# An attention and SwiGLU layer on one core: matmuls of the next stage placed at the seams between stages, and the last output block in two halves

## The chip, the cores and the metric

The kernel runs on one core of one Trainium2 chip. The metric is device microseconds of one execution, as the median of several. Single executions of one kernel differ by up to 5 us here, so the argument rests on two things: timed runs in the same rounds, and the waits of TensorE (PE in the profile) at the seams between the stages, which repeat to about 0.01 us from trace to trace.

## The reference

A transformer block on one sequence of 2,048 tokens with width 1,024, in bfloat16. In short:

```python
mod = (silu(c) @ w_mod)                       # sa, ca, ga, sb, cb, gb
h = layernorm(x) * (1 + ca) + sa
x = x + ga * attention(h)                     # 32 query heads, 4 key/value heads, dim 128,
                                              # the last 512 cached positions, output product with wo
h = layernorm(x) * (1 + cb) + sb
x = x + gb * ((silu(h @ w_gate) * (h @ w_up)) @ w_down)   # inner width 3584
```

## The kernel before

The sequence is worked in two halves (`sc` 0 and 1) of 1,024 tokens, in four stages: attention of half 0, its output product, the same for half 1; then, for each half, rounds of gate-up products and the down product. The large products are done with seven half-size products instead of eight (a Strassen scheme); "product 1" to "product 7" below are these. That needs sums of weights and of activations beforehand, and VectorE (DVE) makes them. A bank is one of the buffers that matmuls add their result into; before it is used anew, ScalarE or VectorE has to empty it. A central helper records every operation, so nearly all matmuls carry one line number (L272) in the profile; the tile names and the time tell them apart.

One attention step is: a part of the query product, the scores of the step before, the exponential on ScalarE (ACT), the product with the values of two steps before, another part of the query product. The seam to the output stage is the last lines:

```python
for i in range(lo, hi + 2):
    ...
    q_first_half(sc, i)              # q products 3, 7, 4, 5 of a group, by i % 4
    scores(i - 1)                    # 4 matmuls of 512 columns; then 2 exponentials of 1024
    pv(i - 2)                        # 16 matmuls of 129 columns
    q_second_half(sc, i)             # q products 2, 1, 6 of the next group
    ...
    if i == hi - 6: start_o(sc)                     # loads output weights, rows 0 to 13
    if i >= hi - 1:                                 # three steps: hi-1, hi, hi+1
        n = 5 * (i - hi + 1)
        for j in range(2):
            o_early(sc, j, n, min(n + 5, 14))       # output rows ahead: 10, 10, 8 matmuls
```

The query products are made in groups of seven, one group for four steps. At the start of the second attention half the products 2, 1, 5, 6 of its first group were made inside the output stage, and product 3 in the first step:

```python
def o_hook0(idx, j):                 # after each column j of output product idx
    ...
    if idx == 6:
        if j == 2:  q_step(1, 0, 2); q_step(1, 0, 1)
        next(hs[0])                                  # activation sums, 1.22 us each on VectorE
        ...
        if j == 3:  q_step(1, 0, 5); q_step(1, 0, 6)
```

A gate-up round (`q` the new weight pair, `pq` the one before). `gmm(bank, n, ...)` is product n, four matmuls; `snap` copies a bank on ScalarE; `g_sum`, `u_sum` add two products on VectorE; `ws(n)` makes n weight sums on VectorE:

```python
if a: gmm(ga, 1, wg); gmm(gb_, 2, wg); snap(sn0, gb_)
if b: gmm(xb, 3, vg); snap(sn1, xb)
if a:
    g_sum(q, 0, ga, sn0)
    if q % FP < 2: ws(2)
if b: gmm(zb, 3, vu); snap(sn2, zb); g_sum(pq, 2, xa, sn1)
if a: g_act(q, 0); gmm(ua, 1, wu); gmm(ub, 2, wu)    # g_act: SiLU on ScalarE
if b: u_sum(pq, 2, za, sn2); g_act(pq, 2)
if a: snap(sn0, ub)
if b: gmm(xa, 7, vg); ...
if a:
    u_sum(q, 0, ua, sn0)
    if q % FP < 2: ws(2)
if b: gmm(za, 7, vu); ...
if a: u_mul(q, 0); ws(2); gmm(ga, 6, wg); gmm(gb_, 5, wg); ...
if b: ...; gmm(xa, 4, vg); ...
if a: gmm(ua, 6, wu); ...
```

The first round of a half has only the `a` lines, the last round only the `b` lines. So in these two rounds, little other work lies between a product and the next product that needs its bank emptied. The weight sums of a half began with its first round (`wsum[0] = w_sums(q0)`). The last block of 512 output columns ended with a multiplication and an addition on VectorE, and then its store.

The softmax here doesn't subtract the row's maximum and nothing guards it: scores larger than these inputs give would overflow.

## Time and profile before

| before | value | where it is read |
|---|---|---|
| median of the first 3 runs | 1167.37 us (1165.66 to 1170.86) | times |
| span of the profiled run | 1164.3 us | page |
| PE busy | 1148.6 us, 99% | page |
| granted PE clock | 1.000 | list of cores |
| matmuls of 512 columns, start to start | 216 ns | trace, consecutive matmul starts |

The page of the kernel before: span, busy time of each engine with its share and its number of instructions, and the shares of the chain of work that ended last.

```profile
span 1164.3 us, 18217 instructions
...
PE 1148.6 (99%) x7087; PEld 585.3 (50%) x7087; DVE 818.1 (70%) x1638; ACT 529.4 (45%) x739; POOL 68.9 (6%) x136
...
PE 91%; DVE 3%; DMA 3%; SPq 1%; ACT 1%; issue 1%; POOL 0%; DVEq 0%; ACTq 0%; POOLq 0%
```

TensorE is the limit. VectorE, the next one, has 30% idle. So only the time that TensorE idles, plus the start and the end, can be won. The waits of PE in the kernel before, in total us, times, and longest:

```profile
PE ps L272 <- POOL arena L406: 2.2, 1, 2.2
PE ps L272 <- DVE arena L829: 2.2, 5, 0.6
PE ps L272 <- ACT arena L799: 2.0, 5, 0.5
PE ps L272 <- DVE arena L821: 1.8, 2, 1.4
PE ps L272 <- DVE arena L900: 1.6, 3, 0.6
```

L829 is an addition that empties a bank, L799 the exponential, L900 a weight sum. To place the waits one goes to the timeline of PE, one line per run of matmuls: start, length, engine, operation, count, and in brackets the idle time before it. First the end of the first attention half:

```profile
236.80 1.45 PE L272 MATMUL ps<-arena 128*128 128x129 bf16 x17
238.76 1.40 PE L272 MATMUL ps<-arena 128*128 128x512 bf16 x16 [0.51 <-ACT arena L799]
```

The scores wait for the exponential. The idle time shown is 0.51 us, but the true loss is larger. The profile models a 512-column matmul as 379 ns long, while they follow each other every 216 ns. The loss is therefore the idle time plus 0.16, that is 0.67 us. All waits in this document, unless said otherwise, are such losses: the spacing of two starts less the usual spacing for that width. Small losses don't break a line of the timeline of PE; there the weight loads (PEld) show them.

The start of the second half, where product 7 waits for an addition:

```profile
342.72 2.10 PE L272 MATMUL ps<-arena 128*128 128x512 f16 x9
345.38 2.43 PE L272 MATMUL ps<-arena 128*128 128x512 f16 x10 [0.55 <-DVE arena L829]
```

The first gate-up round, all engines:

```profile
650.55 0.60 ACT L832 ACTIVATE nsc<-ps 128x512 f32<-128x512 f32 x1 [28.76 <-PE ps L272]
...
651.16 1.28 ACT L1511 ACT_TABLE_LOAD   x1
651.18 0.69 DVE L829 TENSOR_TENSOR arena<-ps,nsc 128x512 f16<-128x512 f32 x1 [0.94 <-PE ps L272]
651.79 0.87 DVE L900 TENSOR_TENSOR arena<-arena 128x512 f16<-128x512 bf16 x2
652.46 0.63 ACT L1511 ACTIVATE arena<-arena 128x512 f16<-128x512 f16 x1
...
652.72 1.90 PE L272 MATMUL ps<-arena 128*128 128x512 f16 x8 [0.48 <-DVE arena L900]
652.99 0.58 ACT L832 ACTIVATE nsc<-ps 128x512 f32<-128x512 f32 x1
653.60 0.69 DVE L829 TENSOR_TENSOR arena<-ps,nsc 128x512 f16<-128x512 f32 x1 [0.94 <-ACT nsc L832]
...
655.14 1.04 PE L272 MATMUL ps<-arena 128*128 128x512 f16 x4 [0.53 <-DVE arena L900]
```

Two waits for weight sums (L900). Behind the second stands another limit: ScalarE loads SiLU's table for 1.28 us, then does the SiLU and a copy, and only then VectorE can add, until 654.29. The last gate-up round of the first half, PE:

```profile
813.67 2.61 PE L272 MATMUL ps<-arena 128*128 128x512 f16 x11
816.76 3.58 PE L272 MATMUL ps<-arena 128*128 128x512 f16 x15 [0.48 <-DVE arena L829]
```

The first gate-up round of the second half (called the twin below), PE:

```profile
909.21 2.48 PE L272 MATMUL ps<-arena 128*128 128x512 f16 x10 [0.58 <-DVE arena L900]
```

And the tail, VectorE:

```profile
1160.82 0.69 DVE L1100 TENSOR_TENSOR tmp<-ps,rowb 128x512 f32<-128x512 f32 x1 [1.60 <-PE ps L272]
1161.55 0.69 DVE L1107 TENSOR_TENSOR arena<-tmp,x_res 128x512 bf16<-128x512 f32 x1
```

### The profile page before, as it was taken

Reading aid. Unit: us, or ns where it says so; the run is one execution under the profiler, and the core shown is the slowest. Engines: PE = TensorE matmul, PEld = TensorE weight load, DVE = VectorE, ACT = ScalarE, POOL = GpSimd, SP = SyncE. Lnnn points to the kernel's source line nnn. Section 1 sums busy time; section 2 is a strip of 40 time slices with the busy share of each in tenths; the row PEclk is TensorE's granted clock in tenths of the full one; section 3 lists DMA queues with packets and bytes.
Section 4 is the critical chain, followed back from the end, with each engine's and each line's share of the span. In section 5 each row is a group of like instructions: output and inputs, shape, how many; then the busy total and the mean of one; then the engine's idle time right before and its main releaser. Section 6 shows DMA issues by size and latency. Waiting matters only on the chain.

```text
span 1164.3 us, 18217 instructions
## 1 busy us (share of the span) xinstructions
PE 1148.6 (99%) x7087; PEld 585.3 (50%) x7087; DVE 818.1 (70%) x1638; ACT 529.4 (45%) x739; POOL 68.9 (6%) x136
## 2 busy tenths in 40 slices
PE   9899999999999999999999999999999999999998
PEld 5565556654446666656444444444444444444443
DVE  4857997657567777686657798777558777776535
ACT  3766777730117777787100354454110444444010
POOL 1100221000000111111000010000000000000000
PEclk9999999999999999999999999999999999999999
DMA  9779899797816888835775332423774423233343
GB/s 331 171 186 200 220 211 223 177 189 203 245 37 148 197 194 205 201 94 130 173 201 163 87 94 73 109 73 100 208 193 151 118 75 107 73 105 129 128 154 109
DMA packets 289765, 179.98 MB, mean 155 GB/s; under 512 B 130448, under 2 KB 277904, under 8 KB 289680
## 3 DMA queue, kind: packets, MB, share of 16 engines
q1 hardware_dynamic: 226736, 92.31, 36.1%
q10 hardware_dynamic: 54304, 55.05, 14.9%
q0 software_dynamic: 8640, 31.46, 8.9%
q8 instruction: 56, 0.92, 0.4%
q14 instruction: 29, 0.24, 0.1%
HBM read 128.45 MB, written 19.92 MB: 127 GB/s over the span
## 4 chain that ended last, share of the span: by engine, by line
PE 91%; DVE 3%; DMA 3%; SPq 1%; ACT 1%; issue 1%; POOL 0%; DVEq 0%; ACTq 0%; POOLq 0%
PE ps L272 91%; DMA arena<-arena 1%; DMA x_res<-in_A_x_dram 1%; DVE arena L829 1%; DMA arena<-in_A_wo_dram 1%; DVE st L413 1%; SPq L382 0%; DVE arena L900 0%; DMA wo_sum<-arena 0%; SPq L341 0%; ACT arena L799 0%; SPq L364 0%; DVE arena L821 0%; ACT nsc L832 0%; SPq L310 0%
## 5 line engine op out<-in xcount | busy, mean ns | idle before, releaser
L272 PE MATMUL ps<-arena 128*128 128x512 f16 (+2 forms) x6782 | 1141.4, 330 | 11.9 <-POOL arena L406 2.2
L272 PEld LDWEIGHTS ps<-arena 128*128 128x128 bf16 (+1 forms) x6782 | 575.0, 98 | 570.6 <-DVE arena L829 9.4
L799 ACT ACTIVATE arena<-ps 128x1024 bf16<-128x1024 f32 x256 | 261.0, 1021 | 49.1 <-PE ps L272 37.2
L832 ACT ACTIVATE tmp<-ps 128x512 f32<-128x512 f32 x166 | 99.1, 597 | 300.8 <-PE ps L272 286.7
L900 DVE TENSOR_TENSOR arena<-arena 128x512 f16<-128x512 bf16 x328 | 133.1, 418 | 3.1
L829 DVE TENSOR_TENSOR arena<-ps,tmp 128x512 bf16<-128x512 f32 (+1 forms) x134 | 91.8, 685 | 46.5 <-PE ps L272 34.5
L821 DVE TENSOR_TENSOR arena<-ps,rl 128x512 f16<-128x512 f32 x128 | 88.5, 691 | 6.0 <-DMA arena<-arena 1.6
L832 ACT ACTIVATE nsc<-ps 128x512 f32<-128x512 f32 x84 | 50.1, 596 | 93.2 <-PE ps L272 90.9
L829 DVE TENSOR_TENSOR arena<-ps,nsc 128x512 f16<-128x512 f32 x84 | 57.3, 686 | 40.4 <-PE ps L272 31.1
L818 DVE RECIPROCAL rl<-ps 128x4 f32<-128x4 f32 x128 | 23.0, 179 | 87.6 <-PE ps L272 86.6
L1038 DVE TENSOR_TENSOR arena<-arena 128x2048 f16<-128x2048 f16 (+3 forms) x56 | 56.0, 1009 | 13.5 <-PE ps L272 12.9
L1511 ACT ACTIVATE arena<-arena 128x512 f16<-128x512 f16 x84 | 49.9, 624 | 30.7 <-DVE arena L829 30.7
L829 DVE TENSOR_TENSOR tmp<-ps,tmp 128x512 f32<-128x512 f32 x32 | 22.0, 689 | 56.4 <-ACT tmp L832 48.3
L832 ACT ACTIVATE arena<-ps 128x512 f32<-128x512 f32 x16 | 9.6, 597 | 93.4 <-PE ps L272 93.4
L950 DVE TENSOR_TENSOR arena<-arena 128x512 f16<-128x512 bf16 x120 | 47.8, 419 | 2.4 <-DMA arena<-in_A_wo_dram 1.4
L413 DVE BATCH_NORM_STATS2 st<-x_res 128x6 f32<-128x512 bf16 x60 | 40.9, 682 | 3.8 <-DMA x_res<-in_A_x_dram 3.4
L1526 DVE TENSOR_TENSOR arena<-arena 128x512 f16<-128x512 f16 x84 | 34.9, 415 | 0.2
L1106 DVE TENSOR_TENSOR tmp<-tmp,rowb 128x512 f32<-128x512 f32 x48 | 33.2, 692 | 1.6
L427 DVE TENSOR_SCALAR nsc<-x_res,mv,rstd 128x1024 f16<-128x1024 bf16 (+1 forms) x30 | 16.1, 538 | 25.2 <-DMA arena<-nsc 24.0
L594 DVE SCALAR_TENSOR_TENSOR arena<-arena 128x1024 bf16<-128x1024 bf16 x24 | 29.1, 1214 | 0.0
L1107 DVE TENSOR_TENSOR arena<-tmp,x_res 128x512 bf16<-128x512 f32 x32 | 22.1, 692 | 1.1
L829 DVE TENSOR_TENSOR arena<-ps,rowb 128x512 f16<-128x512 f32 x28 | 19.3, 689 | 3.9 <-ACT rowb L832 3.9
(86 smaller groups left out, 330.6 us busy)
## 6 DMA issues: line engine op xcount, KB each, us to landing
arena<-in_A_wq_dram SPq DMA_DIRECT2D x28, 512.0 KB, 5.2
arena<-wo_sum ACTq DMA_DIRECT2D x7, 2048.0 KB, 9.1
arena<-in_B_w_gate_dram SPq DMA_DIRECT2D x28, 512.0 KB, 4.0
arena<-in_B_w_up_dram SPq DMA_DIRECT2D x28, 512.0 KB, 5.0
arena<-wd_sum ACTq DMA_DIRECT2D x8, 1792.0 KB, 8.0
arena<-in_B_w_down_dram ACTq DMA_DIRECT2D x6, 1792.0 KB, 7.3
arena<-in_A_wo_dram POOLq DMA_DIRECT2D x16, 512.0 KB, 5.0
wo_sum<-arena POOLq DMA_DIRECT2D x16, 512.0 KB, 4.3
```

What stands on the lines that cost most here:

```text
L272: T.op(PE, lambda: TE.matmul(out_ap, lhsT, rhs, start=start, stop=stop, skip_group_check=skip), reads=reads, writes=[bank_buf])
L413: T.op(DVE, lambda: V.bn_stats(st_[sl][:, hf * 6:hf * 6 + 6], x_res[:, t, hf * 512:hf * 512 + 512]), reads=[B_x[t]], writes=[B_st[sl]])
L799: T.op(ACT, lambda: A.activation(ex_s[es][:, 2 * kp:2 * kp + 2, :], banks2(SCB + 2 * kp), AF.Exp, scale=att_scale), writes=[PB[SCB + 2 * k ...
L821: T.op(DVE, lambda: V.tensor_tensor(o_s[os_].rearrange("p (a b) d -> p a b d", a=2), psap(PVB * 512, [[512, 2], [130, 2], [1, P]]), rlb, A ...
L829: T.op(DVE, lambda: V.tensor_tensor(out, bank(ba), other, ADD), reads=[ob2], writes=[PB[ba], ob])
L832: T.op(ACT, lambda: A.activation(dst, bank(bk), AF.Copy), writes=[PB[bk], db])
L900: T.op(st, lambda: eng.tensor_tensor(o, a, b, op), reads=rd, writes=[wr])
L950: T.op(DVE, lambda: V.tensor_tensor(o, a, b, SUB), reads=rd, writes=[wr])
L1038: T.op(DVE, lambda: V.tensor_tensor(o, a, b, SUB), reads=rd, writes=[sb])
L1106: T.op(DVE, lambda: V.tensor_tensor(tm, tm, rw, MULT), reads=[B_row[row]], writes=[tb])
L1511: T.op(ACT, lambda: A.activation(o, s_, AF.Silu), reads=[sb], writes=[ob])
L1526: T.op(DVE, lambda: V.tensor_tensor(gu[blk][:, p, :], o, s_, MULT), reads=[sb, ob], writes=[B_gu[blk][p]])
```

## The change

The intent is to put matmuls that the next stage needs anyway into the gaps at the seams, and to shorten the tail. Five parts:

1. Attention ends: the 28 early output matmuls are spread over five steps rather than three (4 of them in two earlier steps), and the weights are loaded earlier, in smaller pieces.
2. Start of the second attention half: product 3 of its first group also moves into the output stage, and products 5 and 6 are made there one column earlier, straight after products 2 and 1.
3. First gate-up round of both halves: four weight sums move into the columns of the product before.
4. Last gate-up round of both halves: ten down matmuls are made early (`fill`).
5. The last block of output columns is computed in two halves of 256.

The core of the diff, with cuts:

```diff
             def q_first_half(sc, i):
                 c = i % 4
-                if c < 3:
+                if c < 3 and i != NI:
                     q_step(sc, group_at(sc, i - c), (3, 7, 4)[c])
                 else:
                     q_step(sc, group_at(sc, i + 1), 5)
 ...
-                    if i >= hi - 1:
-                        n = 5 * (i - hi + 1)
-                        for j in range(2):
-                            o_early(sc, j, n, min(n + 5, 14))
+                    if i >= hi - 3:
+                        n = i - hi + 3
+                        o_early(sc, 1, EARLY[1][n], EARLY[1][n + 1])
+                        o_early(sc, 0, EARLY[0][n], EARLY[0][n + 1])
+            EARLY = ((0, 0, 0, 4, 10, 14), (0, 2, 4, 7, 11, 14))
 ...                                                     # o_hook0, idx == 6, j == 2:
                         q_step(1, 0, 2)
                         q_step(1, 0, 1)
+                        q_step(1, 0, 5)
+                        q_step(1, 0, 6)
+                        q_step(1, 0, 3)
 ...                                                     # o_hook1, idx == 6:
+                    if j == 0:
+                        wsum[0] = w_sums(0)
+                    ws(1)
 ...                                                     # gate_up:
-                    if q % FP < 2:
+                    if q % FP == 1:
                         ws(2)
                 if b:
                     gmm(zb, 3, vu, False)
                     snap(*sn[2], zb)
                     g_sum(pq, 2, xa, sn[1])
+                    if fill:
+                        fill(0, 6)
 ...
                     gmm(za, 7, vu, False)
                     u_sum(pq, 3, za, tms[1])
                     g_act(pq, 3)
+                    if fill:
+                        fill(6, 10)
 ...                                                     # seven_products, last product:
+                    if halves and j == TPC - 1:
+                        lo, hi = slice(0, CH // 2), slice(CH // 2, CH)
+                        T.op(ACT, lambda: A.activation(sj[j][0][:, lo], bank(AB[j])[:, lo], AF.Copy), ...)
+                        prod(6, j, BB_[j], True, c=lo)
+                        out(1, j, 0, BB_[j], None, sj[j], lo)
+                        prod(6, j, AB[j], False, c=hi)
+                        out(1, j, 0, AB[j], None, None, hi)
```

More of the change, by code (lines that the diff above doesn't have):

```diff
@@ L1025, in _, with seven_products @@
             ORDER = (1, 2, 6, 5, 3, 7, 4)
-            def seven_products(nk, X, XBf, offs, s1, ver, AB, BB_, out, sj, own_s1, hook, early=(0,) * 4):
+            def seven_products(nk, X, XBf, offs, s1, ver, AB, BB_, out, sj, own_s1, hook, early=(0,) * 4, halves=False):
                 S = {n: [_Buf("S%d_%d" % (n, j)) for j in range(TPC)] for n in (2, 3, 4)}
@@ L1038, in inplace, with prod @@
                         T.op(DVE, lambda: V.tensor_tensor(o, a, b, SUB), reads=rd, writes=[sb])
-                def prod(idx, j, bk, start, k0=0, k1=nk):
+                def prod(idx, j, bk, start, k0=0, k1=nk, c=slice(0, CH)):
                     n = ORDER[idx]
@@ L1049, in prod @@
                             lb = XBf[x][k] if n in (1, 2, 4) else S[{6: 2, 3: 4, 7: 3}[n]][j]
-                        mm(bank(bk), la, va, start and k == 0, k == nk - 1, [lb, vb], PB[bk], skip=True)
+                        mm(bank(bk)[:, c], la, va[:, c], start and k == 0, k == nk - 1, [lb, vb], PB[bk], skip=True)
                 def s1_sum(j):
@@ L1089, in seven_products @@
                 for j in range(TPC):
-                    prod(6, j, AB[j], False)
-                    out(1, j, 0, AB[j], None, None)
+                    if halves and j == TPC - 1:
+                        lo, hi = slice(0, CH // 2), slice(CH // 2, CH)
+                        T.op(ACT, lambda: A.activation(sj[j][0][:, lo], bank(AB[j])[:, lo], AF.Copy), writes=[PB[AB[j]], sj[j][1]])
+                        prod(6, j, BB_[j], True, c=lo)
+                        out(1, j, 0, BB_[j], None, sj[j], lo)
+                        prod(6, j, AB[j], False, c=hi)
+                        out(1, j, 0, AB[j], None, None, hi)
+                    else:
+                        prod(6, j, AB[j], False)
+                        out(1, j, 0, AB[j], None, None)
                     hook(6, j)
@@ L1094, in seven_products, with residual @@
                     arena.regs.append((offs[blk], offs[blk] + nk * KB, S[n]))
-            def residual(t, c0, row, a_bk, b_bk, sj, ring, dst, db, last):
+            def residual(t, c0, row, a_bk, b_bk, sj, ring, dst, db, c=slice(0, CH)):
                 tm, tb = ring
-                rw = rowb[row][:, c0:c0 + CH]
+                tm = tm[:, c]
+                rw = rowb[row][:, c0:c0 + CH][:, c]
                 if b_bk is None and sj is None:
-                    T.op(DVE, lambda: V.tensor_tensor(tm, bank(a_bk), rw, MULT), reads=[B_row[row]], writes=[PB[a_bk], tb])
+                    T.op(DVE, lambda: V.tensor_tensor(tm, bank(a_bk)[:, c], rw, MULT), reads=[B_row[row]], writes=[PB[a_bk], tb])
                 else:
@@ L1104, in residual @@
                         sj = (tm, tb)
-                    add2(tm, tb, a_bk, *sj)
+                    T.op(DVE, lambda: V.tensor_tensor(tm, bank(a_bk)[:, c], sj[0][:, c], ADD), reads=[sj[1]], writes=[PB[a_bk], tb])
                     T.op(DVE, lambda: V.tensor_tensor(tm, tm, rw, MULT), reads=[B_row[row]], writes=[tb])
-                T.op(DVE, lambda: V.tensor_tensor(dst, tm, x_res[:, t, c0:c0 + CH], ADD), reads=[tb, B_x[t]], writes=[db])
+                T.op(DVE, lambda: V.tensor_tensor(dst, tm, x_res[:, t, c0:c0 + CH][:, c], ADD), reads=[tb, B_x[t]], writes=[db])
             class _N1:
@@ L1121, in parts @@
                     return [(0, HP, self.t[:, :, j * P:(j + 1) * P], [self.b[j]])]
-            Q_ver = [[dq("q_ver%d_%d" % (q, i), nc.scalar) for i in range(3)] for q in range(2)]
+            Q_ver = [[dq("q_ver%d_%d" % (q, i), nc.scalar) for i in range(3)] for q in range(3)]
             def loader(sc, raw, sums, nk, kind, places):
@@ L1276, in start_o @@
                 two = [(136 * KB, 9), (117 * KB, 7)] if sc == 0 else [(OFF_E, HP)]
-                places = [[(OFF_WQ, 14), (131 * KB, 2)], [(133 * KB, 12), (OFF_E, 4)]] + [[(o, HP)] for o in (OFF_WQ, OFF_E, OFF_WQ, OFF_N)] + [two]
+                places = [[(OFF_WQ, 7), (OFF_WQ + 7 * KB, 7), (131 * KB, 2)], [(133 * KB, 12), (OFF_E, 4)]] + [[(o, HP)] for o in (OFF_WQ, OFF_E, OFF_WQ, OFF_N)] + [two]
                 wo0[sc] = loader(sc, A_wo, wo_sum, HP, "o", places)
@@ L1296, in attend @@
                     run_bg(1)
+                    if i == hi - 9:
+                        start_o(sc)
                     if i == hi - 6:
-                        start_o(sc)
+                        wo0[sc][0](0, (1,))
                     if i == hi - 1:
-                        wo0[sc][0](0, (1,))
+                        wo0[sc][0](0, (2,))
                         wo0[sc][0](1)
-                    if i >= hi - 1:
-                        n = 5 * (i - hi + 1)
-                        for j in range(2):
-                            o_early(sc, j, n, min(n + 5, 14))
+                    if i >= hi - 3:
[3 more added lines that the diff above has]
+            EARLY = ((0, 0, 0, 4, 10, 14), (0, 2, 4, 7, 11, 14))
             AB_O = (QB, XB, PVB, PVB + 1)
@@ L1320, in out @@
                     ring = rings(tt, j, half)
-                    residual(t, half * CH, 0, a_bk, b_bk, s, ring, x_res[:, t, half * CH:(half + 1) * CH], B_x[t], False)
+                    residual(t, half * CH, 0, a_bk, b_bk, s, ring, x_res[:, t, half * CH:(half + 1) * CH], B_x[t])
                 return out
@@ L1363, in o_hook0 @@
                     hs[0] = h_sums()
+                    next(hs[0])
                 if idx == 6:
@@ L1369, in o_hook0 @@
                         q_step(1, 0, 1)
-                    next(hs[0])
+                        q_step(1, 0, 5)
+                        q_step(1, 0, 6)
+                        q_step(1, 0, 3)
+                    if j < 3:
+                        next(hs[0])
                     if j > 0:
@@ L1373, in o_hook0 @@
                         next(sums2[1], None)
-                    if j == 3:
-                        q_step(1, 0, 5)
-                        q_step(1, 0, 6)
             while bg:
@@ L1456, in o_hook1 @@
                     next(hs[0])
-                if idx == 6 and j < 3:
-                    next(hs[0])
+                if idx == 6:
+                    if j < 3:
+                        next(hs[0])
+                    if j == 0:
+                        wsum[0] = w_sums(0)
+                    ws(1)
             while bg:
@@ L1528, in u_mul, with gate_up @@
                     T.op(DVE, lambda: V.tensor_tensor(gu[blk][:, p, :], bank(bk), s_, MULT), reads=[sb], writes=[PB[bk], B_gu[blk][p]])
-            def gate_up(q, pq):
+            def gate_up(q, pq, fill=None):
                 a = q is not None
@@ L1571, in gate_up @@
                     u_sum(q, 0, ua, sn[0])
-                    if q % FP < 2:
+                    if q % FP == 1:
                         ws(2)
@@ L1600, in gate_up, with f_out, out @@
                         ws(2)
-            def f_out(sc, last):
-                def out(tt, j, half, a_bk, b_bk, s):
+            def f_out(sc):
+                def out(tt, j, half, a_bk, b_bk, s, c=slice(0, CH)):
                     t = (2 * sc + tt) * TPC + j
@@ L1607, in out @@
                     cnt["y"] += 1
-                    residual(t, c0, 1, a_bk, b_bk, s, tms[i % 2], y_b[:, i, :], B_y[i], last)
-                    T.op((Q_out + Q_fin)[i], lambda: SP.dma_start(of[t * P:(t + 1) * P, c0:c0 + CH], y_b[:, i, :]), reads=[B_y[i]])
+                    residual(t, c0, 1, a_bk, b_bk, s, tms[i % 2], y_b[:, i, c], B_y[i], c)
+                    T.op((Q_out + Q_fin)[i], lambda: SP.dma_start(of[t * P:(t + 1) * P, c0:c0 + CH][:, c], y_b[:, i, c]), reads=[B_y[i]])
                 return out
@@ L1613, in _, with f_early @@
                 q0 = sc * FP
+                def f_early(k0, k1):
+                    for k in range(k0, k1):
+                        va, vb = ver(0, k)
+                        mm(bank(0), gu[0][:, k, 0:P], va, k == 0, False, [B_gu[0][k], vb], PB[0], skip=True)
                 if sc == 0:
                     bg.append(stats_task(2 * TPC, 2 * TPC))
-                wsum[0] = w_sums(q0)
                 for r in range(FP + 1):
-                    gate_up(q0 + r if r < FP else None, q0 + r - 1 if r > 0 else None)
+                    gate_up(q0 + r if r < FP else None, q0 + r - 1 if r > 0 else None, f_early if r == FP else None)
                     run_bg(3)
@@ L1646, in f_hook @@
                             hs[0] = h_sums()
+                            wsum[0] = w_sums(FP)
                         next(hs[0])
-                seven_products(FP, gu, B_gu, OFF_GU, m1, ver, (0, 1, 2, 3), (4, 5, 6, 7), f_out(sc, sc == 1), sj, False, f_hook)
+                        ws(1)
+                seven_products(FP, gu, B_gu, OFF_GU, m1, ver, (0, 1, 2, 3), (4, 5, 6, 7), f_out(sc), sj, False, f_hook, (10, 0, 0, 0), sc == 1)
                 if sc == 0:
```

## The prediction

> **What bounds it.** TensorE. The page gives PE 1148.6 us busy of a 1164.3 us span at a granted clock of 1.000; PE is 91% of the chain that ended last. Start-to-start in the trace, a 512-column matmul takes 216 ns, a 129-column one 57, a 256-column one 109, as "N / 2.4 GHz + about 2.5 ns" in the Trainium skill (TensorE: Matmul & The Clock Gate, "Wait — 56ns, not 53.3ns?"). With the program's counts (4,686; 2,048; 24; some small ones) this sums to 1,142 us. Only about 16 us of the PE stream is stall, plus 2.2 us before and 3.5 us after it; 10 us of the stalls lie before 170 us, which the change does not touch. Over 2% is out of reach.
>
> **What is left at the seams** (timeline of PE, spacing beyond those durations):
> - end of each attention half, 238.8 and 548 us: 0.67 each; scores wait for the exponential (ScalarE, 1.02 us, two a step);
> - start of the second attention half, 344.7: 0.71, product 7 waits for the addition that empties its bank;
> - first gate-up round, 652 and 654: 0.64 + 0.69, waiting for weight sums (VectorE, 0.42 each);
> - its second-half twin, 908 and 911: 0.75 + 0.14;
> - last gate-up rounds, 815 and 1071: 0.85 each, 0.77 of it behind the place that gets filled;
> - tail: 3.5 us from last matmul to end: two VectorE operations of 0.69 us, then the store, 1.70 to landing.
>
> **Term by term.**
> 1. Attention ends: the same 28 early output matmuls, spread over five steps. Only the two between scores 61 and 62 shorten the wait: 0.43 each, 0.24 stays. Gain 0.86.
> 2. Second attention half: product 3 moves into the output phase, so the 0.71 goes. But step 64 now takes the else branch, and product 5 of group 0 is computed a second time: 4 added 512-column matmuls (the instruction order shows them), 0.86. Net -0.1 (a loss).
> 3. First gate-up round: four weight sums move ahead, VectorE has 0.9 us idle per column there. The first stall goes. The second then hits ScalarE: a table load (skill, ScalarE: Activation LUTs, "What ACT_TABLE_LOAD costs": about 1283 ns; here 1283), SiLU 0.63, copy 0.58; VectorE's sum ends at 654.30 whatever the weight sums do. 0.56 of 1.33 stays. Gain 0.77.
> 4. Its twin: the last down columns have only 0.47 us of VectorE idle each, and a sum takes 0.43, so the last one pushes the first gate addition by about 0.4. Gain 0.3.
> 5. Last gate-up rounds: 6 + 4 early down matmuls (weights landed 5 us before) cover the stalls; nothing is added. Gain 1.54.
> 6. Last block in halves: two 0.69 operations become two of about 0.42 (estimate: 256-column VectorE operations take 0.35 here), +0.04 for 28 narrow matmuls, the store the same. Gain 0.5.
>
> Sum 3.9 us, all on the PE chain or the tail, 0.3%. 1167.4 - 3.9 = 1163.5; the profiled run before (1166.3) is a little below the median, so 1163.2 us, range 1160.8 to 1166.0. Runs of one kernel spread by 5 us, more than the effect. Chances: faster by over 2% 0.005, within 2% 0.985, slower 0.01.
>
> **What would show it.** PE count +18. Span near 1160.4. Waits at attention ends about 0.24; none over 0.1 at the start of the second half; about 0.5 left at 654, behind the table load; about 0.5 at 908 in two pieces; only the 0.08 in the last rounds; VectorE's last two operations near 0.42.
>
> **What would make it wrong.** Earlier output-weight loads on ScalarE's queue delay an exponential; early sums make VectorE late, so term 4 vanishes; the smaller store lands later; run-to-run spread hides it.

## The result and the profile after

| kernel | runs | median, us | lowest to highest | ratio to before | 95% interval |
|---|---|---|---|---|---|
| before | 6 | 1166.97 | 1165.66 to 1170.86 | | |
| changed | 6 | 1162.97 | 1161.76 to 1165.01 | 0.9963 | 0.9945 to 0.9981 |
| before, second set of rounds | 11 | 1167.54 | 1165.32 to 1169.24 | | |
| changed, second set of rounds | 6 | 1162.33 | 1161.47 to 1164.87 | 0.9959 | 0.9946 to 0.9971 |

The change makes the kernel 0.4% faster, clear of the noise in both sets, and far under 2%.

The kernel was profiled twice. In the first profile (span 1160.2) 86 of 7,105 matmul records are missing; the lines here are from the second, which has all of them. (The profiles of twin_three, no_sums_ahead, no_fill and whole_tail below lack 86 too. All weight loads are there, and where a record is missing next to a wait, 0.216 us is taken off.)

```profile
span 1159.6 us, 18270 instructions
...
PE 1148.7 (99%) x7105; PEld 588.2 (51%) x7105; DVE 819.2 (71%) x1641; ACT 530.9 (46%) x741; POOL 67.6 (6%) x136
...
PE 92%; DVE 3%; DMA 2%; SPq 1%; ACT 1%; issue 1%; POOL 0%; DVEq 0%; ACTq 0%; POOLq 0%
```

PE has 18 more matmuls and its busy time is what it was, while the span fell. The waits of PE that answer to the list above:

```profile
PE ps L272 <- POOL arena L406: 2.2, 1, 2.2
PE ps L272 <- DVE arena L821: 1.5, 2, 1.4
PE ps L272 <- DVE arena L829: 1.3, 5, 0.4
...
PE ps L272 <- ACT arena L799: 0.7, 2, 0.5
```

The line of the weight sums (L900) is gone. The wait for the exponential is smaller by 1.3 us: 1.0 at the two attention ends (0.51 each in this view), the rest at 34 us, where nothing was changed and where waits come and go from run to run. That is why the seams have to be read one by one. The table gives each wait in us, as a loss, from the start-to-start spacing.

| seam | before | changed | gain |
|---|---|---|---|
| end of attention, half 0 and half 1 | 0.67, 0.67 | 0.25, 0.25 | 0.84 |
| start of half 1: product 6, product 7, product 4 | 0, 0.71, 0.09 | 0.15, 0, 0.16 | 0.49 |
| there, matmul time added (4 x 0.216) | | 0.86 | -0.86 |
| first gate-up round: gate, up | 0.64, 0.69 | 0, 0.55 | 0.78 |
| its twin in half 1 | 0.75, 0.14 | 0.29, 0.14 | 0.45 |
| last gate-up round, half 0 | 0.08, 0.64, 0.07, 0.07 | 0.08, 0, 0, 0 | 0.77 |
| last gate-up round, half 1 | 0.08, 0.64, 0.06, 0.06 | 0.08, 0, 0, 0 | 0.76 |
| tail (net of 0.04 for narrow matmuls) | | | 0.63 |

The sum is 3.86 us. (The tail is the time from the last matmul's start to the end, 3.86 before and 3.08 now, less 0.11 for the last matmul's own width and 0.04 that the narrow matmuls add.) An independent reading agrees. All kernels here run the same instructions up to about 210 us, so the stretch from the start of the 1,601st weight load (near 184 us) to the end leaves out the noisy beginning. It lasts 980.01 us before and 976.19 and 976.03 in the two profiles of the changed kernel, 3.8 to 4.0 less. Two more waits after 184 us stand in both kernels and are left out of the table: 0.51 at 501 us and 0.30 to 0.31 in the second gate-up round, at 674 us before and 672 now.

How the lines look now. End of the second attention half, weight loads. The wait of 0.25 us is too short to break the line of the matmuls, but the weight loads, whose idle time has their normal pauses in it as well, show that the exponential ends it:

```profile
547.55 1.88 PEld L272 LDWEIGHTS ps<-arena 128*128 128x128 bf16 x22 [0.58 <-ACT arena L799]
```

The start of the second half, weight loads. The wait of product 7 is gone, and two small ones are there, at product 6 (337.61) and product 4 (346.41), both ended by an addition that empties a bank:

```profile
337.61 0.55 PEld L272 LDWEIGHTS ps<-arena 128*128 128x128 f16 x4 [0.48 <-DVE arena L829]
...
346.41 0.98 PEld L272 LDWEIGHTS ps<-arena 128*128 128x128 bf16 x6 [0.48 <-DVE arena L829]
```

The first gate-up round: the table load is now what the remaining wait stands behind. L829 ends at 653.09 and product 6 starts 0.06 later.

```profile
649.96 1.28 ACT L1529 ACT_TABLE_LOAD   x1
649.97 0.69 DVE L829 TENSOR_TENSOR arena<-ps,nsc 128x512 f16<-128x512 f32 x1 [0.60 <-ACT nsc L832]
...
651.25 0.63 ACT L1529 ACTIVATE arena<-arena 128x512 f16<-128x512 f16 x1
651.79 0.58 ACT L832 ACTIVATE nsc<-ps 128x512 f32<-128x512 f32 x1
652.40 0.69 DVE L829 TENSOR_TENSOR arena<-ps,nsc 128x512 f16<-128x512 f32 x1 [1.74 <-ACT nsc L832]
...
653.15 2.12 PE L272 MATMUL ps<-arena 128*128 128x512 f16 x9 [0.39 <-DVE arena L829]
```

Its twin in the second half, weight loads of the first profile; the addition L829 now ends the wait, not a weight sum:

```profile
906.54 1.41 PEld L272 LDWEIGHTS ps<-arena 128*128 128x128 f16 x8 [0.62 <-DVE arena L829]
```

The last gate-up round of the first half, PE, runs through without a gap that this view shows:

```profile
811.69 8.01 PE L272 MATMUL ps<-arena 128*128 128x512 f16 x36
```

The tail, VectorE, has operations of half the width:

```profile
1156.78 0.42 DVE L1109 TENSOR_TENSOR tmp<-ps,rowb 128x256 f32<-128x256 f32 x1
1157.24 0.42 DVE L1116 TENSOR_TENSOR arena<-tmp,x_res 128x256 bf16<-128x256 f32 x1
```

### The profile page after: what moved, and what is told of

It is laid out like the page before. It is cut to its first block, busy times and chain, and to the rows that moved or that the text cites. A ratio compares the mean times of both kernels' runs of the same rounds, so it can differ in the third digit from the quotient of the medians.

```text
span 1160.2 us, 18184 instructions
## 1 busy us (share of the span) xinstructions
PE 1143.8 (99%) x7019; PEld 588.7 (51%) x7105; DVE 819.0 (71%) x1641; ACT 530.6 (46%) x741; POOL 68.2 (6%) x136
## 4 chain that ended last, share of the span: by engine, by line
PE 95%; DVE 3%; ACT 1%; issue 1%; DMA 1%; SPq 0%; DVEq 0%; ACTq 0%
PE ps L272 95%; ACT arena L799 1%; DMA arena<-in_A_wq_dram 1%; DVE arena L829 1%; DVE st L413 1%; DVE arena L900 0%; DVE arena L678 0%; SPq L341 0%; DVE arena L673 0%; SPq L310 0%; DVE nsc L427 0%; DVE arena L846 0%; PE ps L276 0%; DVE arena L1544 0%; DVE arena L647 0%
## 5 line engine op out<-in xcount | busy, mean ns | idle before, releaser
L900 DVE TENSOR_TENSOR arena<-arena 128x512 f16<-128x512 bf16 x328 | 133.4, 419 | 3.0
L829 DVE TENSOR_TENSOR arena<-ps,tmp 128x512 bf16<-128x512 f32 (+1 forms) x134 | 91.9, 686 | 49.7 <-PE ps L272 38.2
L829 DVE TENSOR_TENSOR arena<-ps,nsc 128x512 f16<-128x512 f32 x84 | 57.4, 687 | 40.8 <-PE ps L272 29.6
L1114 DVE TENSOR_TENSOR tmp<-ps,tmp 128x512 f32<-128x512 f32 x32 | 22.1, 690 | 53.1 <-ACT tmp L832 45.3
L1115 DVE TENSOR_TENSOR tmp<-tmp,rowb 128x512 f32<-128x512 f32 (+1 forms) x49 | 33.6, 686 | 1.7
L1116 DVE TENSOR_TENSOR arena<-tmp,x_res 128x512 bf16<-128x512 f32 (+1 forms) x33 | 22.3, 676 | 1.1
L829 DVE TENSOR_TENSOR arena<-ps,rowb 128x512 f16<-128x512 f32 x28 | 19.3, 689 | 3.9 <-ACT rowb L832 3.4
```

The source lines that it names most:

```text
L829: T.op(DVE, lambda: V.tensor_tensor(out, bank(ba), other, ADD), reads=[ob2], writes=[PB[ba], ob])
L900: T.op(st, lambda: eng.tensor_tensor(o, a, b, op), reads=rd, writes=[wr])
L1115: T.op(DVE, lambda: V.tensor_tensor(tm, tm, rw, MULT), reads=[B_row[row]], writes=[tb])
```

## The experiments

Eight kernels were run for one look each, then three in timed rounds. All gave correct results. Single times say little here, so the verdicts rest on the waits at the seam in question and on the stretch from the 1,601st weight load to the end ("the rest"), 976.0 to 976.2 us for the changed kernel. The runs below come from three chips (chip 5: no_double to silu_ahead; chip 2: twin_three to whole_tail; chip 1: the timed rounds). All edits are against the changed kernel. Each expectation sets two readings against each other, theory A and a rival B. Two things were not undone alone: the move of product 3 (part 2), whose gain is read from the trace, and the earlier loads of part 1. early_none keeps these loads and has the old waits, so at the attention ends they gain nothing by themselves.

### no_double and no_double_again: product 5 once

In the changed kernel, step 64 (`i == NI`, the first of the second attention half) falls into the else branch, which computes product 5 of group 0, already computed a moment before in the output stage.

```diff
-                else:
+                elif i != NI:
                     q_step(sc, group_at(sc, i + 1), 5)
```

> The changed kernel without the second computation of product 5 of group 0 at step 64. Theory A (it is pure added work): 4 matmuls of 512 columns fewer (7,101 in all), no new wait of TensorE over 0.2 us at the start of the second attention half, span about 0.8 us shorter than 1160.2. Rival B (it is a filler that stands where TensorE would wait anyway, for a bank or for the exponential): a wait of 0.6 to 0.9 us appears between the last output product and product 4 of group 0, and the span stays at 1160.2.

Measured: 7,101 matmuls, no new wait at the seam, and product 4 waits 0.09 in place of 0.16. But the span was 1163.0 and the rest 977.13, longer and not shorter. The trace has a single wait of 2.04 us at 579 us, in the output stage. VectorE, timeline of this run:

```profile
580.55 0.55 DVE L427 TENSOR_SCALAR nsc<-x_res,mv,rstd 128x1024 f16<-128x1024 bf16 x1 [1.79 <-DMA arena<-nsc]
```

A normalisation waits for a transposing transfer to leave its buffer, and an addition that TensorE waits for (L1114) comes next on VectorE. In the changed kernel the idle time at this place was 0.19 us. The trace at the seam spoke for theory A, the time against it; so it was repeated.

> The kernel with product 5 once, again: its single run was 1163.0 us, 2.8 above the changed kernel, with a wait of 2.04 us at 579 us that no other profile has at that size. Theory A (that wait is the timing of transfers in that one run, not the edit): 0 to 1.5 us below the changed kernel in the same rounds, and the 2.04 us wait is absent or different in size. Rival B (the edit causes it): slower than the changed kernel by 1 us or more, with the wait at 579 us again near 2 us.

Measured: median 1162.64 (1160.40 to 1165.68, 6 runs), ratio 0.9956 (0.9940 to 0.9972), against 0.9959 for the changed kernel in the same rounds; times can't tell the two apart. The 0 to 1.5 us below the changed kernel that theory A expected did not show in the medians (1162.64 against 1162.33). In its profile the 2.04 us wait is absent and the rest is 975.10 (the first run's 977.13 less 2.04 is 975.09), 0.9 to 1.1 less than the changed kernel: 0.86 of matmuls and 0.07 at product 4. So the second product 5 was pure added work, and the 2 us wait was the timing of transfers in that one run, as far as one repeat can tell. This profile has its own odd wait, 2.67 us at 104 us, behind a late load; more on that at the end.

### early_four and early_none: where the early matmuls count

```diff
-            EARLY = ((0, 0, 0, 4, 10, 14), (0, 2, 4, 7, 11, 14))
+            EARLY = ((0, 0, 0, 4, 10, 14), (0, 0, 4, 7, 11, 14))     # early_four
+            EARLY = ((0, 0, 0, 4, 10, 14), (0, 4, 4, 7, 11, 14))     # early_none
```

> The changed kernel with four early output matmuls between scores 61 and scores 62 and none a step earlier (same 28 in all). Theory A (only matmuls between those two scores count, 0.216 us each): the waits of 0.26 and 0.25 us at the two attention ends go to under 0.05. Rival B (the two placed a step earlier shorten the wait as much as the later two): the total of four is unchanged, so 0.25 stays.

> The changed kernel with all four matmuls a step earlier, before scores 61, and none between scores 61 and 62. Theory A: the wait is back at 0.67 us at each attention end, as before the change. Rival B: 0.25 stays, as the same four stand before scores 62.

Measured: early_four has no wait left at either attention end (below 0.06), rest 975.48. early_none has 0.67 at both. PE at the end of the second half, early_four, one line without a gap:

```profile
545.73 3.94 PE L272 MATMUL ps<-arena 128*128 128x512 bf16 x33
```

and early_none, where the idle time is that of the kernel before:

```profile
548.62 1.73 PE L272 MATMUL ps<-arena 128*128 128x512 bf16 x19 [0.51 <-ACT arena L799]
```

The rest of early_none is 977.37, of which 0.48 is again a wait at 579 us. It is taken for the timing of transfers, as in no_double; this run was not repeated. Theory A holds on both sides: a matmul shortens this wait only if it stands between the scores that the exponential reads and the scores that need its banks. The two that stand a step earlier gained nothing.

### silu_ahead: the table load taken off the path

```diff
             def o_hook1(idx, j):
                 run_bg(1)
+                if idx == 0 and j == 1:
+                    T.op(ACT, lambda: A.activation(acc[:, 0:1], mhalf[:, 0:1], AF.Silu), reads=[B_mh], writes=[B_acc])
```

> The changed kernel with one tiny SiLU on ScalarE in the second output stage, so that the table is loaded there. Theory A (the 0.55 us left in the first gate-up round stands behind the table load of 1.28 us on ScalarE): the wait near 653 us goes to under 0.1. Rival B (it is VectorE's weight sums or the chain sum, SiLU, copy, sum itself): 0.3 to 0.55 stays.

Measured: the wait of 0.55 is gone (below 0.06) and the rest is 975.45, 0.6 to 0.7 less. ScalarE and VectorE in the first gate-up round now follow each other without the 1.28 us:

```profile
651.63 0.63 ACT L1531 ACTIVATE arena<-arena 128x512 f16<-128x512 f16 x1 [0.76 <-DVE arena L829]
...
652.17 0.58 ACT L832 ACTIVATE nsc<-ps 128x512 f32<-128x512 f32 x1
652.78 0.69 DVE L829 TENSOR_TENSOR arena<-ps,nsc 128x512 f16<-128x512 f32 x1 [1.18 <-ACT nsc L832]
```

### twin_three: one weight sum fewer ahead, in the second half

```diff
                         next(hs[0])
-                        ws(1)
+                        if j < TPC - 1:
+                            ws(1)
 ...
                     g_sum(q, 0, ga, sn[0])
+                    if q == FP:
+                        ws(1)
```

> The changed kernel, second half: only three weight sums during the last down columns, the fourth after the first gate addition. Theory A (the fourth sum pushes the gate addition by its 0.42 us, which made the 0.29 us wait at 906 us): that wait goes to under 0.05; the one after it stays between 0 and 0.2. Rival B (the last sum of the activations, 1.22 us, or the copy on ScalarE sets it): 0.29 stays.

Measured: the wait of 0.29 is gone, and the next one is 0.10 in place of 0.14. VectorE around it in the changed kernel (its first profile), where the weight sum L900 stands ahead of the gate addition L829:

```profile
904.34 1.22 DVE L848 TENSOR_TENSOR arena<-arena 128x2048 f16<-128x2048 f16 x1
...
905.47 0.42 DVE L900 TENSOR_TENSOR arena<-arena 128x512 f16<-128x512 f16 x1
905.81 0.68 DVE L829 TENSOR_TENSOR arena<-ps,nsc 128x512 f16<-128x512 f32 x1
```

and in twin_three, where it doesn't:

```profile
904.45 1.22 DVE L848 TENSOR_TENSOR arena<-arena 128x2048 f16<-128x2048 f16 x1
...
905.58 0.68 DVE L829 TENSOR_TENSOR arena<-ps,nsc 128x512 f16<-128x512 f32 x1
```

The addition starts 1.47 us after the start of the activation sum in the one and 1.13 in the other, 0.34 apart. The rest of this run is 976.10, no better than the changed kernel, because 0.4 us were lost at 205 us, in the attention of half 0; the gain of 0.33 at the seam is read from the spacing alone.

### no_sums_ahead and no_fill: single parts undone

no_sums_ahead puts the start of the weight sums back to the first round, in both halves:

```diff
-                    if j == 0:                              # o_hook1; the same in f_hook
-                        wsum[0] = w_sums(0)
-                    ws(1)
 ...
+                wsum[0] = w_sums(q0)
                 for r in range(FP + 1):
 ...
-                    if q % FP == 1:                         # both places in gate_up
+                    if q % FP < 2:
                         ws(2)
```

no_fill drops the ten early down matmuls:

```diff
-                    gate_up(..., f_early if r == FP else None)
+                    gate_up(...)
-                seven_products(..., (10, 0, 0, 0), sc == 1)
+                seven_products(..., (0,) * 4, sc == 1)
```

> The changed kernel with the weight sums back where they were before, in both halves. Theory A: the waits of before return, 0.64 + 0.69 at the first gate-up round and 0.75 + 0.14 at its twin; span longer by about 1.2 us (0.78 + 0.46). Rival B (the gain there came from something else, such as the order of the activations' sums): the waits stay at 0.55 and 0.43.

> The changed kernel without the ten early down matmuls in the last gate-up rounds. Theory A: waits of 0.64, 0.065, 0.065 us return in each, span longer by 1.54 us. Rival B (the moved matmuls only move the wait, into the first down products): under 0.5 us longer.

Measured, no_sums_ahead: waits of 0.64 and 0.69, 0.75 and 0.14; rest 977.26, 1.1 to 1.2 more. Measured, no_fill: waits of 0.64, 0.06, 0.06 in each last round; rest 977.66, 1.5 to 1.6 more. Both as theory A has it. PE of no_fill in the last round of half 0:

```profile
816.40 3.80 PE L272 MATMUL ps<-arena 128*128 128x512 f16 x16 [0.48 <-DVE arena L829]
```

The moved matmuls did not move the wait: nothing new appeared in the down product behind.

### whole_tail: the last block in one piece

```diff
-                seven_products(..., (10, 0, 0, 0), sc == 1)
+                seven_products(..., (10, 0, 0, 0))
```

> The changed kernel with the last block whole. Theory A (the tail is VectorE's two operations): they take 0.69 each in place of 0.42, the tail from the last matmul's start is about 0.6 us longer, the store's time to landing is within 0.15 us of the halved one's. Rival B (the saving is in the smaller store): time to landing 0.3 us or more longer.

Measured: the rest is 976.66, 0.5 to 0.6 more. VectorE's two operations take 0.69 us each (0.42 when halved), 1.42 from start to end against 0.88. The store takes 1.69 us from issue to landing against 1.56. So 0.53 us come from VectorE and 0.13 from the smaller store: mainly A, with a small part of B; the 28 narrow matmuls take back 0.04.

### combined and after_again: the four corrections together

combined is the changed kernel with no_double, early_four, silu_ahead and twin_three. It ran in the same rounds as the changed kernel.

> The changed kernel with four corrections: product 5 once, four early matmuls between scores 61 and 62, SiLU's table loaded in the second output stage, three weight sums ahead in the second half. Theory A (the seams are separate and add up): 0.86 less matmul time, and waits shorter by 0.26 + 0.25 (attention ends), 0.55 (first gate-up round), 0.29 to 0.32 (its twin), 0.07 (product 4): 2.3 us below the changed kernel, 6.2 below the kernel before, ratio near 0.9945. Rival B (a wait removed at one seam comes back at the next, as the whole runs against VectorE or the loads): under 1 us below the changed kernel.

> The changed kernel again, on the same chip as the combined one, for its time. Both theories: ratio to the kernel before 0.9955 to 0.9975; the waits at the seams as in its first profile (0.26, 0.25, 0.16, 0.16, 0.55, 0.29, 0.14, 0.08, 0.08 us), whatever the waits before 200 us do.

| kernel | median, us | lowest to highest | ratio to before | 95% interval | the rest, us |
|---|---|---|---|---|---|
| changed, again | 1162.33 | 1161.47 to 1164.87 | 0.9959 | 0.9946 to 0.9971 | 976.03 |
| combined | 1161.46 | 1159.94 to 1162.52 | 0.9946 | 0.9934 to 0.9958 | 973.69 |

The changed kernel's waits at the seams were those of its first profile to 0.01. In the combined kernel the attention ends and the first gate-up round have no wait left, product 6 keeps 0.15, product 4 has 0.09, the twin 0.11, the last rounds 0.08. Its rest is 2.34 us shorter than that of the changed kernel in the same set, as theory A has it. The waits over 0.05 us that are left in it after 184 us sum to 1.3 us, 0.83 of it the two at 501 and 672 us that no edit touched. In the timed runs the medians differ by 0.9 us, the means by 1.4, and the intervals of the ratios overlap, so the runs alone don't establish that combined is faster than the changed kernel; that it is faster than the kernel before, by 0.5%, they do. For the two profiled executions the traces settle the difference. Their spans, 1158.9 and 1159.6, are only 0.7 us apart because combined took 185.21 us to the 1,601st weight load, 1.7 more than the changed kernel. Most of that lies in one place: from 39.6 to 43.0 us the granted clock was 0.50, and the 25 matmuls from 39.43 us on took about 1.65 us more, start to start, than the same ones in the changed kernel, at full clock. No part of the edit acts there. Whether the unprofiled executions lost time in the same way is open.

## Why the prediction was right

The predicted time was 1163.2 us, the measured median 1162.97. That they agree to 0.2 us is partly luck: the executions of one kernel spread by some 3 to 5 us, and the interval of the ratio allows a gain of 2.2 to 6.4 us. The test of the mechanism is the terms, one by one:

1. **Attention ends: right.** Predicted a gain of 0.86 with 0.24 left each; measured 0.84 with 0.25 left. early_four and early_none show the mechanism.
2. **Second attention half: the direction right, the size not.** The prediction had -0.1, measured is -0.37. The 0.86 for the second product 5 and the 0.71 won were right. The term that failed is "none over 0.1 at the start of the second half": two waits of 0.15 and 0.16 are there. The first is new. Products 2, 1, 5, 6, 3 now follow each other directly. Product 6 uses the bank of product 1, and in the profile of the changed kernel the addition that empties it ends at 337.56, just before the loads for product 6 start at 337.61. Four matmuls of product 5 (0.86 us) lie between; the addition with its start and its release took 0.15 more. Before, a whole column of the output product stood there. The second, at product 4, was 0.09 before and is 0.09 again in both runs of no_double; so 0.07 of it comes with the second product 5. That the first would go with more work between products 1 and 6 was argued and not run.
3. **First gate-up round: right.** Predicted 0.77, measured 0.78, with 0.55 left behind the table load. silu_ahead shows that it is the table load. The Trainium skill (ScalarE: Activation LUTs, "What ACT_TABLE_LOAD costs") gives about 1283 ns for the load; the trace has 1.28 us.
4. **Its twin: mechanism right, size too small.** Predicted 0.3, measured 0.45. The fourth sum does push the gate addition (twin_three), by 0.34 us rather than 0.4, because successive VectorE operations overlap by some 0.08 us in the records; and 0.43 us of waits remain rather than the 0.5 to 0.6 foretold.
5. **Last gate-up rounds: right.** Predicted 1.54, measured 1.53, and no_fill gives them back.
6. **Tail: mechanism right, size a little small.** Predicted 0.5, measured 0.63. The estimate of 0.42 us for a halved operation was met. It agrees with the fit (N + 151) / 0.96 ns that the Trainium skill gives for a float32 addition (VectorE: DVE Perf Modes, "The TRN2 errata — SBUF-src ops pay a fixed extra latency per instruction"): 691 ns at 512 columns, and 424 at 256 as an estimate worked out from it; the traces have 691 to 692 and 424 to 426. The two operations here are near to that addition but not it: one multiplies and reads a bank, the other has a bfloat16 operand. The store was said to take the same and took 0.13 to 0.14 less.

The errors of terms 2, 4 and 6 cancel: 3.9 predicted, 3.86 summed from the seams. That over 2% was out of reach followed from one reading, the PE stream: only 16 us of the span were stalls, 10 of them in a place that the change does not touch.

## What to carry to other kernels

When one engine is busy 99% of the time, list its waits one by one from the spacing of its instructions, and ask of each which operation ends it and which one stands behind that; moved work helps only if it lies between the start of what is waited for and the wait. Count the instructions of a reordered kernel: here four matmuls came in twice, which the correct result doesn't reveal, and they cost more (0.86 us) than the wait that was removed beside them (0.71). When the effect is smaller than the spread of the times, compare the same seam in several profiles rather than the medians.

## What the Trainium skill lacked or had wrong

- TensorE: Matmul & The Clock Gate, "Back-to-back issue gap", gives a sustained roofline of about 131 ns for a matmul of N = 512 in a stream of weight loads and matmuls, and calls 216 ns the isolated gap. Here the sustained spacing over more than 4,600 such matmuls, each with its weight load, is 216 ns, and 57 ns at 129 columns. "Wait — 56ns, not 53.3ns?" on the same page is right.
- ScalarE: Activation LUTs, "What ACT_TABLE_LOAD costs", adds a drain of about 1380 ns to every switch, 2.66 us in all. In this trace the copy before the load ends at 651.15, the load starts at 651.16 and lasts 1.28, and the SiLU starts at 652.46: no drain, a switch cost of 1.3 us.
- DMA: Bandwidth & Descriptors, "Anatomy of one DMA — SWDGE (gpsimd) path", has about 2.0 us of fixed cost, for transfers issued by another engine than here. For SyncE's queue that page has the time to the first byte, but not the time to landing of a small store. The last stores here took 1.69 to 1.71 us from issue to landing at 128 KB and 1.53 to 1.57 at 64 KB.
- No page that was consulted has what limits a comparison of a few microseconds here: waits behind transfers that differ from run to run in the same instructions. The 1,601st weight load started between 183.5 and 186.7 us in 13 profiles, and single waits of 2.67 us (at 104 us), 2.04 (at 579), 1.0 and 0.87 (near 179) each appeared in one profile at that size. The first two stand behind a VectorE operation that waits for a transfer; the others were not followed up.
